# The reciprocals of the softmax sums: from VectorE to GpSimd, as a power

## The chip, the cores and the metric

The kernel runs on one core of a Trainium2 chip. A core has five engines that work side by side, each through its own list of instructions in order: TensorE (PE in the profile, with its weight loads as PEld), VectorE (DVE), ScalarE (ACT), GpSimd (POOL) and SyncE (SP), which here issues most of the DMAs. They wait for one another by semaphores. The metric is the device time of one execution in microseconds (us).

## The reference

Attention that keeps the 32 largest scores of each row, followed by two dense layers with an exact GELU between them:

```python
# q, k, v: (8, 8, 576, 64) float32
scores = scale * np.matmul(q, k.transpose(0, 1, 3, 2))
kth = np.partition(scores, -32, axis=-1)[..., -32:-31]
scores = np.where(scores >= kth, scores, -1000000000.0)
scores = scores - np.max(scores, axis=-1, keepdims=True)
attn = np.exp(scores)
attn = attn / (np.sum(attn, axis=-1, keepdims=True) + 1e-09)
attn_out = np.matmul(attn, v)
# (B, H, S, D) -> x: (4608, 512); w_in: (512, 2048); w_out: (2048, 512)
h = x @ w_in
g = 0.5 * h * (1.0 + erf(h / np.sqrt(2)))
out = g @ w_out
```

The change concerns the division: for each row, one over the sum of the exponentials plus 1e-9.

## The kernel before

The attention is cut into 144 items. An item is two heads (a pair, `e` = 0 and 1) by 128 query rows, so its scores are 128 partitions by 2 x 576 floats, the tile `s`. The per-row numbers of an item lie in a small tile `stat` of 128 x 4 x 2 floats: `neg` (the negated threshold), `bias`, `den` (the sum) and `rden` (one over it).

One loop runs over the items, and in iteration `n` it issues steps of several items, a software pipeline written out by hand (the schedule is manual: the order in the code is the order on each engine). For one item `i` the steps are:

- `scores(i)`: PE multiplies, ACT copies the scores from PSUM to `s`.
- `larger(i)`, `sum_up(i)`, `smaller(i)`: each row of 576 is split into two halves; DVE takes their elementwise maximum (L446), and POOL gets the smaller ones by integer arithmetic as sum (L477) less maximum (L485). Both lists go into the tile `lists`.
- `top_k(i)`: DVE finds the 32 largest by rounds of eight maxima (L513) and replacing them (L516). Between its rounds stands `square_p(n - 2)`, a transpose on DVE (L614) for some items.
- `threshold(i)`: POOL, two operations of 128x2 (L527, L528), `neg` and `bias`.
- `select(i, e)` and `softmax(i, e)`: ACT, a steep Prelu (L547) that pushes all below the threshold down, and Exp (L559), which also sums into `den`.
- `add_small(i)`: POOL adds 1e-9 to `den` (L540).
- `inverse(i)`: DVE makes `rden` with a reciprocal of 128x2 (L534).
- `normalise(i)`: POOL multiplies `s` by `rden` (L582), or, for the first items, makes diagonal matrices of `rden` (L573).
- `transposes(i)`, or a turn through DRAM by DMAs (`write_p`, `read_p`), and `attend(i)`: PE, with ACT copying from PSUM, and the product with v goes to `xT`.

The second half of the kernel, the dense layers, is cut into pieces (`mlp`) that are filled in between on PE: `h_ps` (L820) from `xT` and `w_in`, GELU on ACT (L836), and `y_ps` and `seven` (L920, L938, L941, L974, L976) from `g` and `w_out`. The latter use sums of blocks so that seven products stand for eight; POOL makes those sums (L857 to L860) and adds up the results (L997, L1025 to L1040), ACT copies the seventh product out of its PSUM bank (L992, L995). In most of the run (`few[0]`) that bank, tag `z`, is shared with the scores of the last keys (`t_ps`, `tp_t`, L373), so the copy on ACT frees it for PE.

In iteration `n` POOL's order is: `smaller(n + 1)`, `add_small(n - 1)`, `threshold(n)`, `normalise(n - 1)`, `sum_up(n + 2)`, then the block sums. DVE's order is `top_k(n)`, and behind its last maxima, through the function `last`, `larger(n + 2)` (where `few[0]` holds) and `inverse(n - 1)`. A set `have_larger` keeps `larger` from being issued twice, since the loop also calls `larger(n + 1)` at the head of each iteration.

Of the kernel before, what the change touches and what calls it, by code (L numbers as in the profile page):

```python
# [14 lines left out]
def kernel(  # L15
# [19 lines left out]
    nc = tc.nc  # L35
    f32, i32, u32 = mybir.dt.float32, mybir.dt.int32, mybir.dt.uint32
    bf16, i16, u16 = mybir.dt.bfloat16, mybir.dt.int16, mybir.dt.uint16
    AF = mybir.ActivationFunctionType
    ALU = mybir.AluOpType

    B, H, S, D = q.shape
    P = 128
# [19 lines left out]
    const = ctx.enter_context(tc.tile_pool(name="const", bufs=1))  # L62
# [47 lines left out]
    def flush():  # L110
        held[0] = False
        while late_issues:
            late_issues.pop(0)()
        late_issues.extend(later)
        later.clear()
# [61 lines left out]
    DIAGS = START - 1  # L177
    SINGLE = range(18, 28)
    words = {}
    bounds = const.tile([P, 2], f32, name="bounds")  # L180
    low, high = bounds[:, 0:1], bounds[:, 1:2]
    nc.gpsimd.memset(low, -EXP0 * 2.0**20)
    nc.gpsimd.memset(high, EXP0 * 2.0**-40)

# [71 lines left out]
    for b in range(B):  # L258
# [4 lines left out]
        last = [(b * NP + p, NM) for p in range(0, NP, 2)]  # L263
# [8 lines left out]
    N = len(items)  # L272
# [4 lines left out]
    few = [False]  # L277
# [55 lines left out]
    S_of, stat_of = {}, {}  # L333
# [98 lines left out]
    def paired(i):  # L432

        return PAIRED <= i < N and i not in SINGLE

    def halves_of(i):
        s = S_of[i].rearrange("p (e h n) -> p e h n", e=2, h=2)
        return s[:, :, 0], s[:, :, 1]

    have_larger = set()  # L440

    def larger(i):

        if paired(i) and i not in have_larger:
            have_larger.add(i)
            nc.vector.tensor_tensor(lists_for(i)[:, :, 0], *halves_of(i), op=ALU.max)  # L446

    def into_of(i):

        if i < 2 and i not in into_lists:  # L450
            into_lists[i] = work.tile([P, 2, 2, HS], f32, tag="pt", bufs=1, name="into")
        return into_lists.get(i, lists_of[i])
# [13 lines left out]
    def lists_for(i):  # L466

        if i not in lists_of:
            lists_of[i] = work.tile([P, 2, 2, HS], f32, tag="lists", name="lists")
        return lists_of[i]  # L470
# [10 lines left out]
    def smaller(i):  # L481

        if paired(i):
            both, top = lists_of[i][:, :, 1].bitcast(i32), lists_of[i][:, :, 0].bitcast(i32)
            nc.gpsimd.tensor_tensor(into_of(i)[:, :, 1].bitcast(i32), both, top, op=ALU.subtract)  # L485

    def top_k(i, last, middle):


        stat_of[i] = st = {  # L490
            "first": work.tile([P, 2, 8], f32, tag="first", name="first"),
        }
        stat = work.tile([P, 4, 2], f32, tag="stat", name="stat")
        st.update((n, stat[:, x]) for x, n in enumerate(("neg", "bias", "den", "rden")))
        top = work.tile([P, 2, 16], f32, tag="top", bufs=1, name="top")
        into = [st["first"]] + [
            top[:, :, 8:16] if r == TOPK // 8 - 1 else top[:, :, 0:8] for r in range(1, TOPK // 8)
        ]
        if paired(i):
            t = lists_of[i]  # L500
            u = into_of(i)
            both = u.rearrange("p e h n -> p e (h n)")
            rounds = [(t[:, :, 0], u[:, :, 0]), (u[:, :, 0], u[:, :, 0])]
            rounds = [(*(rounds[r] if 16 * r < TOPK else (both, both)), x) for r, x in enumerate(into)]
        else:
            s = S_of[i].rearrange("p (e n) -> p e n", e=2)
            t = work.tile([P, 2, S], f32, tag="lists", name="rest")
            rounds = [(s if r == 0 else t, t, x) for r, x in enumerate(into)]
        for r, (src, dst, x) in enumerate(rounds):
            if 16 * r == TOPK:  # L510
                middle()
            for e in range(2):
                nc.vector.max(x[:, e], src[:, e])  # L513
            if r < len(rounds) - 1:
                for e in range(2):
                    nc.vector.match_replace(dst[:, e], x[:, e], src[:, e], LOWEST)  # L516
            if r == len(rounds) - 1:
                last()

        st["kth"] = top[:, :, 15]  # L520

    def threshold(i):

        if i < 0 or i >= N:
            return
        st = stat_of[i]
        nc.gpsimd.tensor_scalar(st["neg"], st["kth"], -1.0, None, op0=ALU.mult)  # L527
        nc.gpsimd.tensor_tensor(st["bias"], st["kth"], st["first"][:, :, 0], op=ALU.subtract)  # L528

    def inverse(i):  # L530
        if i < 0 or i >= N:
            return
        st = stat_of[i]
        nc.vector.reciprocal(st["rden"], st["den"])  # L534

    def add_small(i):
        if i < 0 or i >= N:
            return
        st = stat_of[i]
        nc.gpsimd.tensor_scalar(st["den"], st["den"], 1e-9, None, op0=ALU.add)  # L540

    def select(i, e):

        if i < 0 or i >= N:
            return
        st, s = stat_of[i], row(i, e)
        nc.scalar.activation(s, s, func=AF.Prelu, bias=st["neg"][:, e : e + 1], scale=1.0, alpha=STEEP)  # L547
        selected.add((i, e))
# [37 lines left out]
    def squared(i):  # L586

        if not SINGLE.stop - 2 < i < N - 2:
            return False
        if items[i][1] == NM:  # L590
            return i % RINGS != RINGS // 2 - 1
        return moved(i) or (i % 2 == 0 and i % RINGS != 12)
# [17 lines left out]
    def square_p(i):  # L610

        if squared(i):
            s = S_of[i]
            nc.vector.transpose(s, s)  # L614

    def write_p(i):

        if squared(i):
            turned[i] = d = dram.tile([SQ, NJ + NM, P // SQ, P], f32, tag="turned", name="turned")
            s = S_of.pop(i).rearrange("p (x j) -> p x j", j=SQ)  # L620
            d = d.rearrange("i c k n -> i (c k) n")
            for a in range(P // SQ):
                rows = slice(a * SQ, (a + 1) * SQ)
                nc.sync.dma_start(out=d[:, :, rows], in_=s[rows])
# [580 lines left out]
    for n in range(ahead):  # L1205
# [27 lines left out]
        if n > 0:  # L1233
            larger(n + 1)
# [96 lines left out]
            softmax(n - 1, 1)  # L1331
        if n > 0:
            smaller(n + 1)
        add_small(n - 1)
        for piece in tr[-1:] + prep:
            piece(None)
            mlp(1)
# [5 lines left out]
        mlp(left[0])  # L1343
        run_gelus()
        if n < N:
            def last():
                if few[0]:
                    larger(n + 2)
                inverse(n - 1)

            top_k(n, last, lambda: square_p(n - 2))
            write_p(n - 2)
            flush()
            if n == 0:
                larger(1)
        else:
            inverse(n - 1)
        threshold(n)
        if n == 0:
            smaller(1)  # L1360
# [60 lines left out]
```

## Time and profile before

| | |
|---|---|
| Time, median of 3 runs | 1462.1 us (1461.39 to 1462.64) |
| The profiled execution | 1461.3 us, span 1459.5 us, 26550 instructions |
| PE busy | 1442.6 us, 99% |
| DVE busy | 1329.6 us, 91% |
| POOL busy | 1128.4 us, 77% |
| ACT busy | 1056.4 us, 72% |
| Weight loads of PE | 1123.9 us, 77% |

Busy time is given for each engine by itself; the engines overlap. In the rows below, a group of instructions has its line, engine, operation, tiles and shapes, then the count (x144), then the busy time in us and the mean of one in ns, and behind the second bar the idle time just ahead of these instructions with what ended most of it. A row of waits reads "engine, tile, line that waited <- engine, tile, line waited for: us in total, times, longest". A row of a timeline has the start, the duration, the engine, line and operation, and in square brackets the idle time before it and who ended it. A row of stages (`A:B`) has its length and then, for PE, PEld, DVE, ACT and POOL, busy us and the number of instructions, then TensorE's granted clock, the DMA share and GB/s.

### The profile page before, as it was taken

The numbers are of one execution on the slowest core, as the hardware profiler recorded it, in microseconds if no ns is written. First come the engines' busy times: TensorE is split into PE (matmuls) and PEld (weight loads), VectorE is DVE, ScalarE is ACT, GpSimd is POOL, SyncE is SP. The second block draws the span as 40 slices with busy tenths as digits, with TensorE's granted clock in tenths as the row PEclk, the third lists the DMA queues.
The fourth block names the chain that finished last, engine by engine and source line by source line (L and its number), as shares of the span: only waits on it lengthen the run. The fifth ranks groups of instructions, "written<-read, shape, count | busy, mean of one in ns | idle before, by whom it ended". The sixth has DMA issues, their size and how long they took to land.

```text
span 1459.5 us, 26550 instructions
## 1 busy us (share of the span) xinstructions
PE 1442.6 (99%) x8621; PEld 1123.9 (77%) x8621; DVE 1329.6 (91%) x3339; ACT 1056.4 (72%) x1883; POOL 1128.4 (77%) x1290
## 2 busy tenths in 40 slices
PE   8999999999999999999999999999999999999999
PEld 6776678877777777787777778787777777787887
DVE  7999999999999999999999999999999999999601
ACT  7999977777777777767777777777676767677620
POOL 6877657877798878878888878887788887878632
PEclk9999999999999999999999999999999999999999
DMA  7524310045454446456554365456554444543200
GB/s 196 150 87 126 84 48 1 9 98 104 90 113 89 87 87 142 82 113 128 111 99 96 65 117 116 90 112 127 117 102 106 90 80 84 127 98 85 53 15 15
DMA packets 591819, 136.49 MB, mean 94 GB/s; under 512 B 504352, under 2 KB 583232, under 8 KB 591680
## 3 DMA queue, kind: packets, MB, share of 16 engines
q1 hardware_dynamic: 590416, 134.37, 43.5%
q8 instruction: 68, 1.11, 0.3%
q14 instruction: 71, 0.58, 0.1%
q10 hardware_dynamic: 1200, 0.39, 0.1%
q0 software_dynamic: 64, 0.03, 0.0%
HBM read 85.19 MB, written 49.55 MB: 92 GB/s over the span
## 4 chain that ended last, share of the span: by engine, by line
PE 44%; POOL 11%; DVE 7%; issue 3%; ACT 3%; DMA 1%; SPq 0%; DVEq 0%; POOLq 0%; ACTq 0%
PE h_ps L820 17%; PE y_ps L976 11%; PE o L751 5%; PE s_ps L408 3%; POOL s L582 3%; DVE top L513 3%; DVE lists L516 2%; POOL lists L485 2%; POOL lists L477 2%; PE seven L974 2%; PE tp L680 2%; PE y_ps L938 2%; PE y_ps L941 1%; DMA turned<-s 1%; DVE s L614 1%
## 5 line engine op out<-in xcount | busy, mean ns | idle before, releaser
L820 PE MATMUL h_ps<-xT,w_in_sb 128*128 128x256 f32 (+1 forms) x2560 | 533.0, 361 | 0.0
L820 PEld LDWEIGHTS h_ps<-xT,w_in_sb 128*128 128x128 f32 x2560 | 438.9, 191 | 69.2 <-issue 10.9
L513 DVE MAX8 top<-lists 128x8 f32<-128x576 f32 (+1 forms) x792 | 475.9, 641 | 0.0
L547 ACT ACTIVATE s<-s,stat 128x576 f32<-128x576 f32 x288 | 219.2, 786 | 123.0 <-POOL stat L527 122.9
L516 DVE MATCH_REPLACE8 lists<-top,lists 128x288 f32<-128x288 f32 (+1 forms) x528 | 308.0, 589 | 0.0
L582 POOL TENSOR_TENSOR s<-s,stat 128x1152 f32<-128x1152 f32 x135 | 284.8, 2109 | 10.1 <-DVE stat L534 5.3
L559 ACT ACTIVATE s<-s,stat 128x576 f32<-128x576 f32 x288 | 225.2, 787 | 7.6
L485 POOL TENSOR_TENSOR lists<-lists 128x576 int32<-128x576 int32 x132 | 186.6, 1413 | 3.1
L477 POOL TENSOR_TENSOR lists<-s 128x576 int32<-128x576 int32 x133 | 188.2, 1415 | 0.0
L540 POOL TENSOR_SCALAR stat<-stat 128x2 f32<-128x2 f32 x144 | 44.4, 309 | 163.0 <-ACT s L559 156.1
L751 PE MATMUL o<-pt,raw_v 128*64 128x256 f32 x1280 | 152.9, 384 | 1.0 <-ACT pt L685 0.4
L416 ACT ACTIVATE s<-s_ps 128x1024 f32<-128x1024 f32 x127 | 126.4, 1046 | 35.2 <-PE s_ps L408 35.0
L751 PEld LDWEIGHTS o<-pt,raw_v 128*64 128x64 f32 x1280 | 86.8, 136 | 80.9 <-issue 38.1
L976 PE MATMUL y_ps<-w_out_sb,sum 128*128 128x256 f32 x472 | 140.4, 379 | 0.0
L408 PE MATMUL s_ps<-kt,qm 64*128 64x512 f32 x512 | 131.2, 621 | 1.1 <-ACT s L414 0.8
L836 ACT ACTIVATE g<-h_ps 128x512 f32<-128x512 f32 x144 | 78.2, 595 | 66.6 <-PE h_ps L820 66.0
L446 DVE TENSOR_TENSOR lists<-s 128x576 f32<-128x576 f32 x133 | 106.2, 799 | 17.8 <-ACT s L381 5.8
L976 PE MATMUL y_ps<-w_out_sb,g 128*128 128x256 f32 x480 | 116.4, 382 | 0.0
L516 DVE MATCH_REPLACE8 lists<-first,lists 128x288 f32<-128x288 f32 x264 | 114.4, 439 | 0.0
L513 DVE MAX8 first<-lists 128x8 f32<-128x288 f32 x268 | 105.8, 434 | 0.0
L976 PEld LDWEIGHTS y_ps<-w_out_sb,g 128*128 128x128 f32 x480 | 90.4, 190 | 15.0 <-issue 3.1
L976 PEld LDWEIGHTS y_ps<-w_out_sb,sum 128*128 128x128 f32 x472 | 89.8, 190 | 12.1
(162 smaller groups left out, 2359.0 us busy)
## 6 DMA issues: line engine op xcount, KB each, us to landing
turned<-s SPq DMA_DIRECT2D x272, 144.0 KB, 3.6
pt<-turned SPq DMA_DIRECT2D x272, 144.0 KB, 3.2
raw_v<-in_v_dram SPq DMA_DIRECT2D x64, 128.0 KB, 2.5
raw_q<-in_q_dram SPq DMA_DIRECT2D x112, 72.0 KB, 2.3
raw_k<-in_k_dram SPq DMA_DIRECT2D x112, 72.0 KB, 2.4
out_dram<-y SPq DMA_DIRECT2D x30, 256.0 KB, 3.1
w_out_sb<-in_moe_w_in_dram SPq DMA_DIRECT2D x14, 511.8 KB, 4.9
w_out_sb<-in_moe_w_out_dram SPq DMA_DIRECT2D x10, 511.8 KB, 4.1
```

Source lines behind the costliest of these rows:

```text
L408: nc.tensor.matmul(s_ps[:, e], lhsT=q_t[rows, :], rhs=kt[rows, main_keys(pair)], start=True, stop=True)
L416: nc.scalar.activation(spread(s, S + TL, SM), s_ps, func=AF.Copy, scale=scale)
L477: nc.gpsimd.tensor_tensor(t[:, :, 1].bitcast(i32), a.bitcast(i32), b.bitcast(i32), op=ALU.add)
L485: nc.gpsimd.tensor_tensor(into_of(i)[:, :, 1].bitcast(i32), both, top, op=ALU.subtract)
L513: nc.vector.max(x[:, e], src[:, e])
L516: nc.vector.match_replace(dst[:, e], x[:, e], src[:, e], LOWEST)
L547: nc.scalar.activation(s, s, func=AF.Prelu, bias=st["neg"][:, e : e + 1], scale=1.0, alpha=STEEP)
L559: nc.scalar.activation(s, s, func=AF.Exp, bias=st["bias"][:, e : e + 1], scale=1.0, accum_out=st["den"][:, e : e + 1],)
L582: nc.gpsimd.tensor_tensor(s, s, wide, op=ALU.mult)
L751: nc.tensor.matmul(o[e * D : (e + 1) * D, 0:n], lhsT=vt[:, j, e, :], rhs=pt[:, e * NJ + j if j < NM else NM, :], start=(j == 0), stop=(j = ...
L820: nc.tensor.matmul(h_tile(u)[:, i, :], lhsT=w_in_sb[:, ko, f * P : (f + 1) * P], rhs=xT[:, ko, c0 : c0 + n], start=(ko == 0), stop=(ko == ...
L976: nc.tensor.matmul(acc[names][:, k], lhsT=lhsT, rhs=rhs, start=(j == 0 and k == 0), stop=(j == FT // 2 - 1 and k == 1),)
```

## The change

`inverse` moves from DVE to POOL. It takes in the addition of the small constant, and directly behind it POOL raises the sum to the power of minus one, with a column of -1.0 that is set once at the start and read with a step of zero. It stands where `add_small` stood, ahead of the threshold. With no reciprocal behind the top 32, the function `last` and the set `have_larger` go; `larger(n + 2)` is then issued at the head of the next iteration, as `larger(n + 1)` there, and there is nothing else between on DVE. DVE, PE, ACT and SP keep the order of everything else.

```diff
-    bounds = const.tile([P, 2], f32, name="bounds")
+    bounds = const.tile([P, 3], f32, name="bounds")
+    minus = bounds[:, 2:3]
     low, high = bounds[:, 0:1], bounds[:, 1:2]
...
+    nc.gpsimd.memset(minus, -1.0)
...
-    have_larger = set()
-
     def larger(i):
-        if paired(i) and i not in have_larger:
-            have_larger.add(i)
+        if paired(i):
             nc.vector.tensor_tensor(lists_for(i)[:, :, 0], *halves_of(i), op=ALU.max)
...
-    def top_k(i, last, middle):
+    def top_k(i, middle):
...
-            if r == len(rounds) - 1:
-                last()
...
     def inverse(i):
         if i < 0 or i >= N:
             return
         st = stat_of[i]
-        nc.vector.reciprocal(st["rden"], st["den"])
-
-    def add_small(i):
-        if i < 0 or i >= N:
-            return
-        st = stat_of[i]
         nc.gpsimd.tensor_scalar(st["den"], st["den"], 1e-9, None, op0=ALU.add)
+        nc.gpsimd.tensor_tensor(
+            st["rden"], st["den"],
+            bass.AP(tensor=minus.tensor, offset=minus.offset, ap=[list(minus.ap[0]), [0, 2]]),
+            op=ALU.pow,
+        )
...
-        add_small(n - 1)
+        inverse(n - 1)
...
-            def last():
-                if few[0]:
-                    larger(n + 2)
-                inverse(n - 1)
-
-            top_k(n, last, lambda: square_p(n - 2))
+            top_k(n, lambda: square_p(n - 2))
...
-        else:
-            inverse(n - 1)
```

## The prediction

> **What bounds the kernel now.** I read the page's head first, then the busy time by stage, then who waits for whom, and then the timelines of POOL, ACT and PE at the places where a later POOL could reach PE.
>
> ```profile
> span 1459.5 us, 26550 instructions
> ```
>
> ```profile
> core 0: us, PE busy (x) PEld busy (x) DVE busy (x) ACT busy (x) POOL busy (x), PEclk, DMA share, GB/s
> 0.00:100.00 100.00, 89.88 (x681) 72.28 (x682) 91.14 (x252) 90.21 (x152) 75.04 (x83) 1.00 0.54 158
> 100.00:1385.00 1285.00, 1282.01 (x7603) 990.73 (x7603) 1233.70 (x3077) 953.02 (x1705) 1033.77 (x1180) 1.00 0.46 93
> ```
>
> ```profile
> 665.41 4.32 PE h_ps L820 x20
> 1398.06 6.91 PE h_ps L820 x32
> ```
>
> From 100 to 1385 us PE is busy for 1282.0 of 1285 us at the full granted clock (1.00). A busy PE may still be stretched by late operands, so the last fence, two pieces of the chain that ended last, compares its pace in the middle with the tail, where it has nothing to wait for: 4.32 / 20 and 6.91 / 32 are both 0.216 us for a 128x256 matmul. PE is the bound after the first 100 us, and what an edit gives there is at most the 3.0 us in which PE is idle. DVE is close behind (1233.7 us, 96%), POOL has 1285 - 1033.8 = 251 us left, about 1.9 us for each of the roughly 134 items in this stretch. In the first 100 us PE is not the bound; there ACT scales the weights too (90.2 us busy) and DVE has 91.1.
>
> ```profile
> POOL stat L540 <- ACT s L559: 156.1, 65, 5.7
> ACT s L547 <- POOL stat L527: 122.9, 45, 6.2
> ...
> POOL stat L527 <- DVE top L513: 40.3, 49, 3.0
> ...
> DVE stat L534 <- POOL stat L540: 27.8, 27, 6.2
> ```
>
> This is the loop that the change touches. POOL's addition (L540) waits for ACT's Exp sums; POOL's threshold (L527) stands behind it and waits for DVE's top 32; ACT's selection (L547) waits for the threshold 45 times. DVE's reciprocal waits 27 times for the addition.
>
> **What leaves DVE.** 144 reciprocals and the waits before them (the groups of instructions that matter below, and the reciprocal with the longest wait):
>
> ```profile
> L534 DVE RECIPROCAL stat<-stat 128x2 f32<-128x2 f32 x144 | 22.7, 158 | 31.1 <-POOL stat L540 27.8
> L528 POOL TENSOR_TENSOR stat<-top,first 128x2 f32<-128x2 f32 x144 | 55.9, 388 | 0.0
> L582 POOL TENSOR_TENSOR s<-s,stat 128x1152 f32<-128x1152 f32 x135 | 284.8, 2109 | 10.1 <-DVE stat L534 5.3
> ```
>
> ```profile
> 1382.06 0.17 DVE L534 RECIPROCAL stat<-stat 128x2 f32<-128x2 f32 x1 [6.21 <-POOL stat L540]
> ```
>
> 144 x 0.158 = 22.7 us of work and 31.1 us of idle time, 53.8 us, but the longest of the waits, 6.2 us, is the last item's, when DVE has no top 32 left to do. I cost the rest at nothing gained, because PE is the bound: DVE would come to its maxima earlier and wait there for ACT's copies of PE's scores. Should DVE be what PE waits for, the first rival below has the price. The order of the other DVE work stays: the pairwise maximum (L446) for item n+2 stood behind the top 32 of item n and stands there still, only issued at the head of the next iteration. The normalising multiplication (L582) loses its wait for DVE (5.3 us, last row of the first fence); in its place it waits for the power, which on POOL's queue has long been done, as the threshold stands between. What is late next there is the multiplication's own queue, POOL.
>
> **What comes to POOL.** 144 powers of 128x2 behind the additions, one memset at the start, no DMA. POOL works in order: behind each power stand the threshold, the normalising multiplication, the integer sums for a later item and the small sums of the second matrix product. No power is in the trace. The nearest row is L528, also a two-input f32 operation of 128x2 on POOL: 0.388 us in the mean, 0.185 at the least (first row below). For a lower bound I take 0.185, since a power can't do less than a subtraction; the longest POOL operation of 128x2, 1.312 us (second row), is the upper bound, though nothing here excludes more. I take 0.39, the mean of the nearest row. Between two dependent POOL operations lie 0.08 us: L540 starts at 591.04, takes 0.75, and L527 starts at 591.87 (rows below). So one power moves what stands behind it by e = 0.39 + 0.08 = 0.47 us; the bounds are 0.27 and 1.39.
>
> The Trainium skill, "GPSIMD Engine Reference", section "Engine selection", speaks against the move: elementwise work belongs on VectorE, and GpSimd takes about twice as long for two inputs. By it the power would be 2 x 0.158 = 0.32 us (an estimate), e 0.40 and the sum below 5.3 us in place of 6.6; L528's 0.388 against the reciprocal's 0.158 is a worse ratio than that, and the row decides.
>
> ```profile
> L528 POOL TENSOR_TENSOR stat<-top,first x144: 185/197/675, 19.4 to 1375.9; 128x2 f32<-128x2 f32 x144
> L527 POOL TENSOR_SCALAR stat<-top x144: 218/218/1312, 18.2 to 1375.7; 128x2 f32<-128x2 f32 x144
> ```
>
> 144 x 0.47 = 68 us more in POOL's queue, and most of it lies in waits: where L540 waited for ACT (65 times) or L527 for DVE (49 times) a later POOL finds that time again. It counts where POOL ran without a gap up to a threshold for which ACT waits, and where PE then has no room. I went through the 45 places and compared the end of ACT's copy of `seven`, which frees a PSUM bank, with the start of the next matmul in that bank. Most have room to spare. These don't (times in us, timelines of POOL, ACT and PE).
>
> Kind A, three times (ACT's selection at 592.12, its twin, and the last at 1276.50):
>
> ```profile
> 581.93 0.22 POOL L540 TENSOR_SCALAR stat<-stat 128x2 f32<-128x2 f32 x1 [2.53 <-ACT s L559]
> 591.04 0.75 POOL L540 TENSOR_SCALAR stat<-stat 128x2 f32<-128x2 f32 x1
> 591.87 0.22 POOL L527 TENSOR_SCALAR stat<-top 128x2 f32<-128x2 f32 x1
> 592.12 1.44 ACT L547 ACTIVATE s<-s,stat 128x576 f32<-128x576 f32 x2 [3.62 <-POOL stat L527]
> 595.84 0.38 ACT L995 COPY p<-seven 128x256 f32<-128x256 f32 x1
> 596.27 0.49 PE L373 MATMUL tp_t<-kt,qm 128*128 128x128 f32 x2 [0.31 <-ACT p L995]
> 1276.50 1.44 ACT L547 ACTIVATE s<-s,stat 128x576 f32<-128x576 f32 x2 [3.62 <-POOL stat L527]
> ```
>
> POOL has no wait from 581.93 to the threshold at 591.87, so two powers lie in it; ACT runs on without a gap to 596.22 (L995: 595.84 + 0.38), and PE waits for that already. Each costs 2e = 0.94 us, three cost 2.8.
>
> Kind B, three times (first 419.56, last 1103.95):
>
> ```profile
> 419.56 1.44 ACT L547 ACTIVATE s<-s,stat 128x576 f32<-128x576 f32 x2 [6.16 <-POOL stat L527]
> 741.76 0.22 POOL L540 TENSOR_SCALAR stat<-stat 128x2 f32<-128x2 f32 x1
> 750.55 0.22 POOL L540 TENSOR_SCALAR stat<-stat 128x2 f32<-128x2 f32 x1
> 751.21 0.22 POOL L527 TENSOR_SCALAR stat<-top 128x2 f32<-128x2 f32 x1 [0.45 <-DVE top L513]
> 760.65 0.22 POOL L540 TENSOR_SCALAR stat<-stat 128x2 f32<-128x2 f32 x1
> 761.56 1.44 ACT L547 ACTIVATE s<-s,stat 128x576 f32<-128x576 f32 x2 [6.15 <-POOL stat L527]
> 765.28 0.38 ACT L995 COPY p<-seven 128x256 f32<-128x256 f32 x1
> 765.79 0.41 PE L373 MATMUL tp_t<-kt,qm 128*128 128x128 f32 x2
> 1103.95 1.44 ACT L547 ACTIVATE s<-s,stat 128x576 f32<-128x576 f32 x2 [6.15 <-POOL stat L527]
> ```
>
> Three powers in a row without a wait for ACT; the wait for DVE at 751.21 gives back 0.45 - 0.08 = 0.37, and PE has 765.79 - 765.66 = 0.13 of room: 3e - 0.50 = 0.91 us each, 2.7 in all.
>
> Kind C, five times (first 457.09, last 1141.47):
>
> ```profile
> 457.09 1.44 ACT L547 ACTIVATE s<-s,stat 128x576 f32<-128x576 f32 x2 [3.81 <-POOL stat L527]
> 724.30 1.44 ACT L547 ACTIVATE s<-s,stat 128x576 f32<-128x576 f32 x2 [3.80 <-POOL stat L527]
> 728.03 0.38 ACT L995 COPY p<-seven 128x256 f32<-128x256 f32 x1
> 728.66 0.38 PE L373 MATMUL tp_t<-kt,qm 128*128 128x128 f32 x2
> 1141.47 1.44 ACT L547 ACTIVATE s<-s,stat 128x576 f32<-128x576 f32 x2 [3.80 <-POOL stat L527]
> ```
>
> One power, as the one before it falls into a wait for DVE, and 728.66 - 728.41 = 0.25 of room: e - 0.25 = 0.22 us each, 1.1 in all. One more place has as little room; it lies within the rounding below.
>
> The cover everywhere else is POOL's wait for ACT, whose pace PE sets; it is gone when the powers between two such waits outgrow it, first ahead of kind A, where four powers meet the 2.53 us at 581.93 (at e above 0.7).
>
> **The sum.** 2.8 + 2.7 + 1.1 = 6.6 us, 7 with the place left out. The profiled execution took 1461.3 us, 1.8 us around the span of 1459.5; the median of the three runs is 1462.1, and within their spread the two agree. Added to the median: 1469.1, so 1469. With e = 0.27 the same sum is 2.7 us, with 1.39 it is 25, and 33 when the lost cover ahead of kind A (4e less 2.8, three times) is added. A measurement here tells apart about 0.2%, 2.9 us.
>
> **Rivals.** Faster: DVE, not PE's own work, holds the last percent, and the power disappears in POOL's waits. DVE no longer stands behind POOL's addition, the thresholds that waited for DVE (49 times, 40.3 us) come earlier, and the selections with them. It can give back at most PE's 3.0 us of idle time and in the first 100 us ten reciprocals and their 1.0 us of waits, 2.6 us (the row below; 10 x 0.158 + 1.0): 1462.1 - 5.6 = 1456.5. It decides if e stays under the room that PE has in kinds B and C, or if those thresholds turn out to be held by DVE. Against it speaks that in kinds A to C POOL had no gap ahead of the threshold, or a short one. Chance 0.18.
>
> ```profile
> DVE stat L534 <- POOL stat L540: 1.0, 3, 0.5
> ```
>
> No change: the power costs hardly more than a subtraction without contention (0.185 to 0.2), 2.7 us by the sum, and some of that is won back on DVE: 1462 to 1465. For it speaks the median of L528, 0.197. Chance 0.22.
>
> My forecast, a power of 0.2 to 0.7 us: 1465 to 1476 (e = 0.78 gives 13, and 14 with the lost cover). Chance 0.40.
>
> A long power, 0.7 to 1.3 us, computed in many steps: 1476 to 1497, with the cover ahead of kind A gone. Chance 0.13.
>
> POOL becomes the bound: from e = 1.9 us on the idle time of each item is used up. At the length of POOL's costliest group, L582 with 2.109 us, e is 2.19 and 134 x 0.3 = 40 us are the least, since not every wait can be filled: 1502 and more. Chance 0.07.
>
> **How the numbers follow.** Faster is the first rival, 0.18; same is the second, 0.22; slower are the last three, 0.60. The range from 1457.5 to 1490 leaves out the end of the first rival and about half of the last two, under 2 in 10.
>
> **What would show it.** Right: a POOL group of 144 two-input 128x2 operations at about 0.39 us; DVE busy some 23 us less and idle more, before its pairwise maxima; selections that wait longer for the threshold at the places of kinds A to C, and PE's waits for the copy of `seven` longer by 0.2 to 0.9 us there and nowhere else. Wrong: a power far from 0.39 us, or PE's waits at these places unchanged or gone.

## The result, and the profile after

The changed kernel takes 1479.74 us in the median of 4 runs (1479.61 to 1480.43), before 1461.92 (4 runs, 1461.39 to 1462.64). The ratio is 1.0123, 95% interval 1.0108 to 1.0138: 17.8 us slower. 1469 was forecast; the sign and the range held, the size is more than twice the forecast. The profiled execution has a span of 1477.9 us, 18.4 more than before.

The page's busy times, and the row of the stage from 100 to 1385 us (its columns as before):

```profile
PE 1447.3 (98%) x8621; PEld 1121.4 (76%) x8621; DVE 1333.2 (90%) x3195; ACT 1057.8 (72%) x1883; POOL 1220.5 (83%) x1435
```

```profile
100.00:1385.00 1285.00, 1268.87 (x7504) 973.43 (x7503) 1228.03 (x2920) 942.35 (x1683) 1106.12 (x1296) 1.00 0.45 92
```

PE does the same 8621 matmuls. It is idle for 1477.9 - 1447.3 = 30.6 us, before for 1459.5 - 1442.6 = 16.9: 13.7 us of the 18.4. The other 4.7 are not longer matmuls: their durations add up to 3145.0 us, before 3144.6. A matmul's record overlaps the next one's (1702.1 us of overlap before, 1697.7 now, in which the ends of matmuls are modelled), and behind a wait there is nothing to overlap with. POOL has 92.1 us more work (1220.5 - 1128.4). DVE has no less: 22.7 us of reciprocals are gone, and its busy time is 3.6 us higher. DVE's order changed in one thing more than the reciprocals: at three places between 127 and 153 us an operation on the weights (`w_out_sb`, `w_sum`) now stands ahead of the maximum; PE starts nowhere later there.

The groups of instructions with their shapes say why (count | busy us, mean ns | idle before):

```profile
L445 DVE TENSOR_TENSOR lists<-s 128x576 f32<-128x576 f32 x133 | 122.6, 923 | 35.0 <-ACT s L383 23.6 <-ACT s L394 1.0
L532 POOL TENSOR_TENSOR stat<-stat,bounds 128x2 f32<-128x2 f32 x144 | 111.5, 775 | 12.0
L531 POOL TENSOR_SCALAR stat<-stat 128x2 f32<-128x2 f32 x144 | 51.3, 356 | 149.6 <-ACT s L555 142.5
```

L532 is the power: 0.775 us in the mean, where 0.39 was taken. L445 is DVE's pairwise maximum (L446 before), now 0.923 us in the mean. Its row of before:

```profile
L446 DVE TENSOR_TENSOR lists<-s 128x576 f32<-128x576 f32 x133 | 106.2, 799 | 17.8 <-ACT s L381 5.8
```

Who waits for whom (us in total, times, longest); line numbers are lower by 1 to 9 behind the removed lines (L543 was L547, L524 was L527, L512 was L513, L991 was L995), and L375 was L373:

```profile
ACT s L543 <- POOL stat L524: 152.1, 54, 6.7
POOL stat L531 <- ACT s L555: 142.5, 63, 5.7
...
DVE lists L445 <- ACT s L383: 23.6, 26, 2.2
...
PE tp_t L375 <- ACT p L991: 12.4, 16, 1.6
DVE top L512 <- POOL stat L525: 11.2, 16, 1.8
...
PE tp_t L656 <- POOL diag L569: 5.2, 4, 1.6
...
PE tp_t L662 <- POOL s L578: 1.0, 3, 0.3
...
POOL stat L524 <- DVE top L512: 6.5, 9, 3.0
```

ACT's selection waits 152.1 us for POOL's threshold (122.9 before). POOL's wait for DVE's top 32 ahead of the threshold was 40.3 us, 49 times; 6.5 us are left, so that reserve is used up. PE waits 16 times for the copy of `seven`, 12.4 us, where it waited three times before (kind A, 0.31 us each):

```profile
PE tp_t L373 <- ACT p L995: 1.0, 3, 0.3
```

The maxima now wait for ACT's copies (23.6 us in place of 5.8): DVE did come earlier, and it waits there.

The timelines of POOL, ACT and PE at kind A (the place that was 592.12 before):

```profile
586.68 0.22 POOL L531 TENSOR_SCALAR stat<-stat 128x2 f32<-128x2 f32 x1 [0.72 <-ACT s L555]
586.98 0.72 POOL L532 TENSOR_TENSOR stat<-stat,bounds 128x2 f32<-128x2 f32 x1
587.67 0.22 POOL L524 TENSOR_SCALAR stat<-top 128x2 f32<-128x2 f32 x1
...
596.49 0.61 POOL L531 TENSOR_SCALAR stat<-stat 128x2 f32<-128x2 f32 x1
597.19 0.71 POOL L532 TENSOR_TENSOR stat<-stat,bounds 128x2 f32<-128x2 f32 x1
597.88 0.23 POOL L524 TENSOR_SCALAR stat<-top 128x2 f32<-128x2 f32 x1
...
598.14 1.44 ACT L543 ACTIVATE s<-s,stat 128x576 f32<-128x576 f32 x2 [4.90 <-POOL stat L524]
601.87 0.38 ACT L991 COPY p<-seven 128x256 f32<-128x256 f32 x1
602.30 0.49 PE L375 MATMUL tp_t<-kt,qm 128*128 128x128 f32 x2 [1.60 <-ACT p L991]
```

Two powers stand between POOL's last wait (0.72 us, at 586.68) and the threshold at 597.88. From the start of one power to the threshold are 597.88 - 597.19 = 0.69 us, so one power moves the queue by e = 0.69, not 0.47. PE's wait at this place was 0.31 us and is 1.60: 1.29 more, close to 2e = 1.38. Kinds B and C, and four places that were not among the eleven of the sum (the last waits for the normalisation), from PE's timeline:

```profile
774.78 0.49 PE L375 MATMUL tp_t<-kt,qm 128*128 128x128 f32 x2 [1.39 <-ACT p L991]
735.89 0.49 PE L375 MATMUL tp_t<-kt,qm 128*128 128x128 f32 x2 [0.35 <-ACT p L991]
251.13 0.49 PE L375 MATMUL tp_t<-kt,qm 128*128 128x128 f32 x2 [0.61 <-ACT p L991]
387.69 0.49 PE L375 MATMUL tp_t<-kt,qm 128*128 128x128 f32 x2 [0.48 <-ACT p L991]
445.85 0.49 PE L375 MATMUL tp_t<-kt,qm 128*128 128x128 f32 x2 [0.22 <-ACT p L991]
581.90 0.33 PE L662 MATMUL tp_t<-ident,s 128*128 128x128 f32 x1 [0.32 <-POOL s L578]
```

### The profile page after: what moved, and what is told of

Read it like the earlier page. It is cut to its first block, busy times and chain, and to the rows that moved or that the text cites. A ratio compares the mean times of both kernels' runs of the same rounds, so it can differ in the third digit from the quotient of the medians.

```text
span 1477.9 us, 26767 instructions
## 1 busy us (share of the span) xinstructions
PE 1447.3 (98%) x8621; PEld 1121.4 (76%) x8621; DVE 1333.2 (90%) x3195; ACT 1057.8 (72%) x1883; POOL 1220.5 (83%) x1435
## 4 chain that ended last, share of the span: by engine, by line
PE 67%; POOL 15%; ACT 8%; DMA 3%; issue 3%; SPq 2%; DVE 1%; POOLq 0%; DVEq 0%; ACTq 0%
PE h_ps L816 24%; PE y_ps L972 13%; PE o L747 7%; PE s_ps L410 5%; PE tp L676 3%; POOL s L578 3%; PE seven L970 2%; PE y_ps L934 2%; POOL lists L484 2%; PE y_ps L916 2%; PE y_ps L937 2%; POOL lists L476 2%; ACT s L543 2%; ACT s L555 1%; POOL stat L531 1%
## 5 line engine op out<-in xcount | busy, mean ns | idle before, releaser
L512 DVE MAX8 top<-lists 128x8 f32<-128x576 f32 (+1 forms) x792 | 476.4, 642 | 8.7 <-POOL stat L525 8.6
L543 ACT ACTIVATE s<-s,stat 128x576 f32<-128x576 f32 x288 | 218.9, 784 | 152.1 <-POOL stat L524 152.1
L484 POOL TENSOR_TENSOR lists<-lists 128x576 int32<-128x576 int32 x132 | 190.6, 1444 | 3.1
L531 POOL TENSOR_SCALAR stat<-stat 128x2 f32<-128x2 f32 x144 | 51.3, 356 | 149.6 <-ACT s L555 142.5
L445 DVE TENSOR_TENSOR lists<-s 128x576 f32<-128x576 f32 x133 | 122.6, 923 | 35.0 <-ACT s L383 23.6
L532 POOL TENSOR_TENSOR stat<-stat,bounds 128x2 f32<-128x2 f32 x144 | 111.5, 775 | 12.0
L512 DVE MAX8 first<-lists 128x8 f32<-128x288 f32 x268 | 106.7, 438 | 0.0
```

## The experiments

Two theories stood against each other, and a third between them. The **queue theory**: POOL's power delays the threshold behind it, the selection on ACT waits, and PE with it; DVE's relief is worth nothing. The **DVE theory**: what costs is the changed order on DVE, where the reciprocal no longer stands behind the top 32. The third, "work" in the expectations: POOL's added time costs by its length, wherever it stands. The queue theory fell in the third experiment, in the form that only work ahead of the threshold costs.

**The multiplication in the power's place** (POOL multiplies the sum by the column; the reciprocal is left out).

```diff
-            op=ALU.pow,
+            op=ALU.mult,
```

> The changed kernel with a multiplication in place of the power: the same tiles and place, but the sums are only negated, so the reciprocal is left out. Queue theory (the loss is the length of the operation behind the addition, which delays the threshold, ACT's selection and PE's next matmul in the bank of seven): the multiplication takes about 0.2 us instead of 0.72, so e is 0.2 to 0.45 and the sum over the eleven places 2 to 7 us: 1463 to 1469 us. Rival DVE (the loss comes from what happens on DVE without the reciprocal: the pairwise maximum that is slowed down from 799 to 923 ns and the new wait for the threshold, 11 us): most of the 17.8 us stay, 1472 us or more. Rival work (144 more operations in POOL's queue, wherever they stand): in proportion to their time, 1465 to 1469 us.

1466.28 us, ratio 1.0028 (1.0018 to 1.0039). The group of this kernel:

```profile
L532 POOL TENSOR_TENSOR stat<-stat,bounds 128x2 f32<-128x2 f32 x144 | 38.8, 269 | 12.0
```

A multiplication of the same shape takes 0.269 us in the mean. The power's length alone, on the same place, is worth 1479.74 - 1466.28 = 13.5 us. The queue theory (1463 to 1469 us) and the work theory (1465 to 1469) both had this time, so it does not part them; the DVE theory had 1472 or more.

**No operation in the power's place** (the addition writes `rden`; the reciprocal is left out).

```diff
-        nc.gpsimd.tensor_scalar(st["den"], st["den"], 1e-9, None, op0=ALU.add)
-        nc.gpsimd.tensor_tensor(
...
+        nc.gpsimd.tensor_scalar(st["rden"], st["den"], 1e-9, None, op0=ALU.add)
```

> The changed kernel without any power: POOL's addition writes straight into the tile that the normalising multiplication reads, so the reciprocal is left out and POOL and DVE both have less to do. Queue theory: 1460 to 1463 us, no change against the kernel before, because PE is the bound and the 53.8 us that DVE gains in work and waits are worth nothing. Rival DVE: 1470 us or more. A third reading, that DVE's relief is worth something and the power only hides it: 1455 to 1459 us.

1463.99 us, ratio 1.0013 (1.0004 to 1.0022). DVE without reciprocals, POOL as before: nothing is gained, rather 1.9 us lost, and the time is 1 us above the 1460 to 1463 of the queue theory. The pairwise maximum of this kernel shows where DVE's 22.7 us went:

```profile
L445 DVE TENSOR_TENSOR lists<-s 128x576 f32<-128x576 f32 x133 | 124.9, 939 | 25.9 <-ACT s L383 11.9 <-ACT s L394 3.3 <-DVE top L512 0.5
```

18.7 us more than in before (106.2) are spent in the maximum itself, and 8 us more in waits ahead of it (25.9 against 17.8).

**Addition and power behind the threshold.**

```diff
-        inverse(n - 1)
...
         threshold(n)
+        inverse(n - 1)
...
         normalise(n - 1)
```

> The changed kernel with the addition and the power moved behind the threshold on POOL, ahead of the normalising multiplication. Queue theory: the threshold no longer stands behind its neighbour's power; at kind A one power instead of two lies in the path and the addition of 0.3 to 0.8 us leaves it, so 1460 to 1465 us. Rival work: the operations and POOL's busy time are the same, 1476 to 1480 us. Rival DVE: DVE's instructions are the same, 1472 us or more.

1475.08 us, ratio 1.0091 (1.0076 to 1.0106): a miss. With nothing of the sums ahead of the threshold, the queue theory had this kernel near before, 1460 to 1465 us; the 1476 to 1480 of the work theory come within 1 us. The waits and groups of this kernel:

```profile
POOL stat L524 <- DVE top L512: 90.9, 62, 3.6
...
PE tp_t L375 <- ACT p L991: 5.0, 6, 1.3
...
PE tp L676 <- ACT xT L752: 3.0, 4, 0.8
...
PE tp_t L662 <- POOL s L578: 1.9, 3, 0.6
```

```profile
L524 POOL TENSOR_SCALAR stat<-top 128x2 f32<-128x2 f32 x144 | 63.4, 440 | 90.9 <-DVE top L512 90.9
L525 POOL TENSOR_TENSOR stat<-top,first 128x2 f32<-128x2 f32 x144 | 56.5, 392 | 0.0
```

And the threshold's groups of the changed kernel:

```profile
L524 POOL TENSOR_SCALAR stat<-top 128x2 f32<-128x2 f32 x144 | 41.1, 286 | 10.0 <-DVE top L512 6.5 <-DMA turned<-s 3.6
L525 POOL TENSOR_TENSOR stat<-top,first 128x2 f32<-128x2 f32 x144 | 35.0, 243 | 0.0
```

POOL now waits for DVE ahead of the threshold, 90.9 us in place of 6.5; in the changed kernel the addition and the power ran in that time. The thresholds cost more besides (63.4 + 56.5 = 119.9 us, in the changed kernel 41.1 + 35.0 = 76.1): they start at the end of DVE's top 32, when its next maximum starts. Of the 144 L524, 117 overlap with a maximum here, 43 in the changed kernel, and such a one takes 0.49 us in the mean, the others 0.24. PE waits less for the copy (5.0 us against 12.4), and more for the normalisation, which comes later (1.9 us against 1.0), and for ACT's copies into `xT` (L676, 3.0 us against 0.5).

**A power too many in the kernel before** (POOL raises the sum as well, into a spare tile; DVE keeps its reciprocal and its order).

```diff
...
         nc.gpsimd.tensor_scalar(st["den"], st["den"], 1e-9, None, op0=ALU.add)
+        nc.gpsimd.tensor_tensor(spare, st["den"], ..., op=ALU.pow)
```

> The kernel before, reciprocal on DVE and all, with an added power on POOL behind the addition whose result nobody reads. Queue theory: the delay of the threshold is the same as in the changed kernel, 1476 to 1482 us. Rival DVE (the loss comes from the reciprocal being gone from DVE): 1462 to 1466 us. Rival work: 1476 to 1482 us.

1481.55 us, ratio 1.0133 (1.0117 to 1.0148). The whole loss is there with DVE's part untouched: the DVE theory falls (the queue and the work theory both had 1476 to 1482). What the changed kernel has besides, DVE's relief, is worth 1.8 us at this load, less than the two intervals tell apart.

**A second power in the changed kernel**, into a spare tile.

> The changed kernel with a second power behind the first, whose result nobody reads. Queue theory: the shift of the threshold doubles from 0.69 to 1.38 us; by the prediction's sum 8.3 + 10.9 + 5.7 us at kinds A, B and C, and 4 x 1.38 - 2.8 = 2.7 us three times for the lost cover, 33 us, times 1.36 (measured 15.7 against the summed 11.6 us at 0.69) 45 us over the 1464.0 us without any power: 1500 to 1515 us. Rival work (a fixed price for each us of POOL's work, 26.7 us for each us of a power's length between the multiplication and the power): 1479.7 + 0.69 x 26.7 = 1498 us. A rival in which only the place of one power counts: 1482 us or less.

1534.83 us, ratio 1.0506 (1.0492 to 1.0520): a miss of all three forecasts, which were too low. The second power costs 55 us, over three times the first (15.8 us against no power). Not all of it is waiting: of the 54.3 us that the span is longer than the changed kernel's, PE is idle for 38.4 and busy for 15.9 with the same matmuls, at a granted clock of 0.993 in place of 1.000 (last section). The middle of this kernel, 640 to 980 us, and who waits:

```profile
640.00:980.00 340.00, 326.24 (x1877) 249.64 (x1875) 315.23 (x752) 231.62 (x421) 308.89 (x371) 0.99 0.50 100
```

```profile
ACT s L549 <- POOL stat L525: 219.8, 73, 7.4
...
PE tp_t L376 <- ACT p L997: 28.9, 18, 2.9
...
POOL stat L525 <- DVE top L513: 3.7, 2, 3.0
```

POOL is busy for 308.9 of 340 us, and the selection waits for it 73 times.

**Only the power behind the threshold.** After the third experiment the queue theory was revised: POOL's time counts wherever it stands, and its place decides a part.

```diff
+    def power(i):
...
         threshold(n)
+        power(n - 1)
...
         normalise(n - 1)
```

> The changed kernel with the addition left ahead of the threshold and only the power behind it, ahead of the normalising multiplication. Queue theory as first stated: each threshold has one power less ahead of it, so A counts one power, B two, C none: 2.1 + 2.6 + 0 = 4.7 us over 1464, 1468 to 1471 us. Revised theory after the addition and the power behind the threshold gave 1475.1 us: POOL's queue is so full that time spent waiting for DVE ahead of the threshold is lost if the power no longer fills it, and the normalising multiplication is late instead; then 1471 to 1477 us.

1472.69 us, ratio 1.0077 (1.0063 to 1.0091), as the revised theory had it, and 1.7 us above the first form's bound. Against the kernel with no power (1463.99) the power costs 8.7 us here and 15.8 in front of the threshold: somewhat over half stays when it no longer stands ahead of its own iteration's threshold. The thresholds of later iterations still stand behind it in POOL's queue, so this does not part a delayed threshold from work alone.

**Addition and reciprocal both on DVE.**

```diff
+        nc.vector.tensor_scalar(st["den"], st["den"], 1e-9, None, op0=ALU.add)
         nc.vector.reciprocal(st["rden"], st["den"])
...
-        add_small(n - 1)
```

> The opposite of the change: the kernel before with the addition moved to DVE too, directly ahead of the reciprocal; POOL makes neither. Queue theory: the threshold on POOL loses an operation of 0.22 to 0.75 us ahead of it and no longer stands behind ACT's sums; PE's waits at kind A (0.31 us and what starting again costs) go, DVE has 144 x 0.16 = 23 us more, which lie in its slack: 1459 to 1462 us. Rival DVE (DVE at 96% of the middle is the bound in truth): 1464 to 1480 us.

1471.34 us, ratio 1.0067 (1.0055 to 1.0080): a miss, and the wrong sign. The rival of that expectation, DVE as the bound in truth, had it (1464 to 1480). Its stage, and one wait:

```profile
100.00:1385.00 1285.00, 1274.70 (x7541) 982.20 (x7541) 1255.60 (x3208) 947.77 (x1693) 1009.35 (x1036) 1.00 0.46 93
```

```profile
POOL stat L527 <- DVE top L513: 175.1, 91, 4.6
```

POOL has less to do and waits for DVE 91 times. DVE is busy for 1255.6 of 1285 us; 23 us more, 144 additions of 0.160, did not fit there either. So more work on DVE costs, though taking work from it gives nothing.

**No addition at all** (before, with DVE's reciprocal straight from the sums). The largest score's exponential is 1, so a sum is at least 1, and 1e-9 is less than half of the last place of such a float32 number.

```diff
-        add_small(n - 1)
```

> The kernel before without the addition of 1e-9: DVE takes the reciprocal straight from ACT's sums (each sum holds an exponential of zero, so it is at least 1 and the constant is under half a step of float32). Queue theory: POOL's queue is 44 us shorter in all and the threshold has no operation ahead of it: 1458 to 1461 us. If the wait for ACT's sums on DVE takes the place of the one on POOL: 1462 us, no change.

1457.37 us, ratio 0.9972 (0.9960 to 0.9983): faster than both kernels, by 4.1 us against before in its own comparison. Its stage and its waits:

```profile
100.00:1385.00 1285.00, 1283.59 (x7625) 994.04 (x7625) 1232.34 (x3077) 956.05 (x1708) 1014.09 (x1046) 1.00 0.46 93
```

```profile
POOL stat L527 <- DVE top L513: 172.0, 82, 4.9
ACT s L547 <- POOL stat L527: 104.9, 40, 5.6
```

PE is busy for 1283.6 of 1285 us. Against the kernel with both on DVE, the one difference is DVE's addition: 23.1 us of DVE's time cost 14.0 us.

**The power alone** (the changed kernel without the addition).

```diff
-        nc.gpsimd.tensor_scalar(st["den"], st["den"], 1e-9, None, op0=ALU.add)
         nc.gpsimd.tensor_tensor(
```

> After without the addition of 1e-9: POOL takes the power straight from the sums, DVE makes no reciprocal. Queue theory: ahead of the threshold stands one instruction of 0.69 us of queue where before had the addition of about 0.39, so e is about 0.3 in place of 0.69 and POOL works some 73 us more than before instead of 112 minus the additions: 1464 to 1468. If it is the power's own length that costs, wherever the queue stands (work on POOL that DVE and PE are held up by), 1470 or more.

1469.37 us, ratio 1.0050 (1.0037 to 1.0062): above the one forecast, at the edge of the other. By itself it decides nothing; it is a point of the table below.

**Neither addition nor reciprocal** (the normalisation multiplies by the sums; the reciprocal is left out).

```diff
-        nc.vector.reciprocal(st["rden"], st["den"])
+        st["rden"] = st["den"]
...
-        add_small(n - 1)
```

> Before without the addition and without the reciprocal (the normalisation multiplies by the sums; the reciprocal is left out): the fourth cell beside before (both), the kernel without DVE's reciprocal (1464.0) and the kernel without POOL's addition (1457.4). If DVE's reciprocal costs nothing where it stands, 1457 to 1460. If DVE's 22 us were a cost of their own, 1455 or less.

1459.24 us, ratio 0.9981 (0.9972 to 0.9989). As expected if the reciprocal costs nothing on DVE: with it the kernel is no slower (1457.37), just as the kernel before is no slower (1461.9) than the one without reciprocal but with the addition (1463.99).

**No addition, and the reciprocal ahead of the maximum for item n+2 on DVE.**

```diff
             def last():
+                inverse(n - 1)
                 if few[0]:
                     larger(n + 2)
-                inverse(n - 1)
```

> The kernel without POOL's addition, with DVE's reciprocal put ahead of the selection's first maximum instead of behind it. DVE's reciprocal then is ready for POOL earlier but waits for ACT's sum with the maximum behind it. If the normalisation's lateness bounds, 1455 to 1457; if DVE's queue does, 1458 to 1462.

1464.39 us, ratio 1.0018 (1.0009 to 1.0027): 7 us more than with the reciprocal behind, and beyond both forecasts. Its wait and its maximum:

```profile
DVE stat L534 <- ACT s L559: 28.7, 25, 2.9
```

```profile
L446 DVE TENSOR_TENSOR lists<-s 128x576 f32<-128x576 f32 x133 | 121.5, 914 | 7.6 <-ACT s L381 2.7 <-DVE stat L534 1.2
```

The reciprocal waits 25 times for ACT's sums, and now the maximum stands behind that wait; with the reciprocal behind, it waited nearly as long (27.2 us, 24 times), but behind the maximum. The maximum itself is slower too, 0.914 us in the mean in place of 0.832, 11.0 us in all. Which of the two carries the 7 us was not separated.

**POOL's work for the sums, and the time.** The kernels that differ only in what POOL does for the sums ahead of the threshold, and in DVE's reciprocal, by the busy time of that work on POOL in their profiles:

| Work on POOL for the sums | busy us | on DVE | ratio to before |
|---|---|---|---|
| none | 0 | none | 0.9981 |
| none | 0 | reciprocal | 0.9972 |
| addition | 45.6 | none | 1.0013 |
| addition (before) | 44.4 | reciprocal | 1 |
| addition, multiplication | 84.2 | none | 1.0028 |
| power | 116.4 | none | 1.0050 |
| addition, power (the change) | 162.8 | none | 1.0123 |
| addition, power into a spare tile | 166.0 | reciprocal | 1.0133 |
| addition, two powers | 279.5 | none | 1.0506 |

Taken along the kernels without a reciprocal, and times 1462, the first 116 us cost 10 us, 0.09 us for each; the next 46 cost 0.23 each, the next 117 cost 0.48 each, of which 15.9 / 117 = 0.14 is PE's longer busy time, for the larger part by the lower clock (last section). There is no plain price for a microsecond on POOL: it rises as the waits are used up.

## Why the prediction was wrong, and what held

**The bound and DVE's relief: right.** PE was the bound, and taking the reciprocal from DVE gave nothing: 1.8 us less with the power on POOL, 1.9 us more on each of the two bases without it. The freed time went into the waits of the maxima, as argued, and into the maxima themselves, which was not foreseen (below). With this the first rival fell. What came is the rival of the long power, 1476 to 1497 us with a chance of 0.13, and near its lower end. Its condition, a power of 0.7 to 1.3 us, was met, but that its time came out is in part luck: the lost cover ahead of kind A, which it names, is not what cost. Of these 2.53 us 0.72 are left; only 1.81 were used, where four powers would have taken 4 x 0.69 = 2.76. And the prediction's sum with such an e stays below 1476 (next but one paragraph).

**The mechanism and its places: right, as far as the sum went.** The copy of `seven` is what PE waits for, at kinds A, B and C as named. 2e, 3e - 0.50 and e - 0.25 with the measured e of 0.69 give 1.38, 1.57 and 0.44 us. The waits grew by 1.29, 1.39 and 0.35; with what PE loses when it starts again after a wait, the places cost 1.28, 1.61 and 0.61 us (steps from one matmul's start to the next in both timelines of PE, the table below).

**The first step that failed: the power's duration,** "I take 0.39, the mean of the nearest row". It is 0.775 in the mean, 0.717 in the median. A subtraction of the same shape was the nearest row, but not the nearest operation. The prediction's own sum with e = 0.69 is 3 x 1.38 + 3 x 1.57 + 5 x 0.44 = 11.0 us in place of 6.6, so 4.4 of the 11.8 us that were missing in the span (18.4 less 6.6). The 0.08 us between operations, added to the power's length, was a second error the other way: addition and threshold, on which it was read, do not depend on each other, and the threshold starts 0.025 us before the power's record ends. The Trainium skill's rule, "GPSIMD Engine Reference", section "Engine selection", was about two times DVE's duration for two inputs. The power's 0.775 us are 4.9 times the reciprocal's 0.158, the multiplication's 0.269 are 1.7 times (all means); no run has a two-input operation of this shape on DVE, so the trace bears the rule out only roughly for the multiplication, and a power is far from it.

**The second step that failed, and the larger: "Most have room to spare",** with which the sum put all other places at nothing ("there and nowhere else"). The same 8621 matmuls stand in the same order in both profiles, so the 18.4 us can be laid out by place, from how much each step from one matmul's start to the next grew (with the few matmuls right behind each place):

| Where PE starts later | places | us |
|---|---|---|
| Kind A, copy of `seven` | 3 | 3.8 |
| Kind B, copy of `seven` | 3 | 4.8 |
| Kind C, copy of `seven` | 5 | 3.1 |
| Copy of `seven`, elsewhere (251.13, 387.69, 445.85 and two like the last) | 5 | 2.7 |
| Normalisation (L662) | 3 | 1.7 |
| Diagonal matrices of the first items (L656) | the first items | 1.1 |
| Transposes behind ACT's copy into `xT` (L676) | 2 | 0.9 |
| All else | | 0.3 |

The eleven places of the sum hold 11.7 us, 0.7 more than the sum with the measured e; the places at nothing hold 6.7. Most are the same mechanism at places with a little more room (387.69 is the one left to the rounding), the others are waits for work on POOL and ACT that comes later than before.

**What stands behind both.** The step "most of it lies in waits" took the waits on POOL as a cover of fixed size. The second power, the power behind the threshold and the power alone fit a cover that is shared and runs out. POOL's time costs something wherever it stands (8.7 us behind the threshold), and more ahead of it (15.8). That it costs the more the less is left of the 40.3 us that POOL waited for DVE is read from these runs, not tested by itself. That the two parts, the threshold's delay and the rest, add up in just this way for every place was not measured.

**Left open.** Whether the kernel is truly better off with a reciprocal on DVE than without (1.9 us on both bases without a power, one of the two with intervals that overlap), and why, is not settled. A candidate stands in the rows: on both bases the maxima take longer without it (18.7 us in all with the addition, 17.1 without, 0.960 us in the mean against 0.832). The new wait of DVE for POOL (L512 for L525, 11.2 us) may come from `top` having one buffer; a second one was not tried.

## What to carry to other kernels

An operation that the trace doesn't show should be priced by its kind and not by its shape, and where its price decides the sign of an edit, it is worth a run of its own. Beside a full engine, an engine at 77% has no free 23%: its waits are what others lean on, and a microsecond on it cost from 0.09 to 0.48 us here (the last with a lower clock in it), the dearer the more was added. Before an operation is moved, ask whether it is needed: leaving out the addition of 1e-9 to sums that are at least 1 gave 4.1 us, where no place that was tried for the reciprocal gave anything.

## What the runs showed of the hardware

A power of 128x2 elements on POOL takes 0.717 us in the median, the addition ahead of it 0.223 (rows of the changed kernel; least, median and longest in ns), and the multiplication in the power's place 0.195 (the row of that kernel). The means are higher because of overlaps with DVE's maximum, below: the 47 powers that overlap with one take 0.90 us in the mean, the other 97 take 0.71.

```profile
L532 POOL TENSOR_TENSOR stat<-stat,bounds x144: 707/717/1364, 26.2 to 1402.3; 128x2 f32<-128x2 f32 x144
L531 POOL TENSOR_SCALAR stat<-stat x144: 218/223/765, 25.9 to 1402.0; 128x2 f32<-128x2 f32 x144
```

```profile
L532 POOL TENSOR_TENSOR stat<-stat,bounds x144: 194/195/857, 26.3 to 1388.4; 128x2 f32<-128x2 f32 x144
```

DVE's two-input maximum and operations of POOL hold each other up: in the two cases below the one that starts second takes longer. The timelines of the changed kernel, and then DVE's of the kernel before at the addition of kind A (591.04, 0.75 us):

```profile
576.52 1.41 POOL L484 TENSOR_TENSOR lists<-lists 128x576 int32<-128x576 int32 x1
577.23 1.32 DVE L445 TENSOR_TENSOR lists<-s 128x576 f32<-128x576 f32 x1
```

```profile
590.95 0.76 DVE L446 TENSOR_TENSOR lists<-s 128x576 f32<-128x576 f32 x1
```

Started at 577.23 beside a POOL operation that ends at 577.93, the maximum takes 1.32 us and ends 0.62 behind that one, as if nearly all of it had waited. In the kernel before it started first, at 590.95, took 0.76 and ended at 591.71; there POOL's addition, which takes 0.22 elsewhere, waited in its place and ended at 591.79, after 0.75 us. The Trainium skill, "GPSIMD Engine Reference", section "Specifications", says that GpSimd shares its SBUF interfaces with VectorE and contends with DVE instructions with two SBUF inputs; the trace agrees, and gives the size. In the changed kernel the 27 maxima that start beside no operation of POOL take 0.757 us in the mean, the 41 that start beside POOL's subtraction (L484) 1.22; those that start beside a 128x2 operation already under way are hardly slower (0.76 to 0.78). In the kernel before only 12 start beside that subtraction. So DVE's freed time was given back: its maxima were issued where they met POOL's long operations, 0.923 us in the mean instead of 0.799.

TensorE's granted clock fell in the kernel with two powers. Its four executions had 0.992 to 0.993 in the mean, the changed kernel's four 0.998 to 1.000. Its six longest waits for the copy of `seven`, at kinds A and B, take 2.87 to 2.89 us, and 0.3 to 0.7 us behind the end of each the clock goes to half for 3.4 us. The first, from PE's timeline, and its stage:

```profile
434.03 0.54 PE L376 MATMUL tp_t<-kt,qm 128*128 128x128 f32 x2 [2.88 <-ACT p L997]
```

```profile
434.40:437.70 3.30, 3.30 (x14) 2.83 (x12) 1.72 (x4) 3.09 (x7) 2.09 (x4) 0.50 0.43 159
```

Six times 3.4 us at half speed are worth about 10 us (an estimate, 6 x 1.7). In the profiled execution of the changed kernel, whose waits at these places are 1.6 us at most, the clock shows no such drop. That the waits cause it, and from what length on, was not tested.
